# Batch 1 of an attention and MLP kernel: another split of k's subtraction, casts of v ahead of k's exponentials, products half a block later, batch 3's v loaded ahead of its q

## The chip, the cores and the metric

The kernel runs on one core of one Trainium2 chip. The metric is the device time of one execution in microseconds (us). The engines are named as the profile names them: PE multiplies matrices (PEld is its loading of weights), DVE is VectorE, ACT is ScalarE, POOL is GpSimd, and SP is SyncE, which here only issues transfers.

## What is computed

Linear attention on q, k and v of 8 batches, 8 heads, 576 rows and 64 columns, and a two-layer perceptron on its output:

```python
q_s = exp(q - max(q, axis=-1));  q_s = q_s / sum(q_s, axis=-1)
k_s = exp(k - max(k, axis=2));   k_s = k_s / sum(k_s, axis=2)     # axis 2: the rows
kv   = einsum('bhsd,bhse->bhde', k_s, v)
attn = einsum('bhsd,bhde->bhse', q_s, kv)
x    = attn, (batch, row) as 4608 tokens, (head, column) as 512 features
h    = x @ w_in                    # 512 to 2048
out  = maximum(0.01 * h, h) @ w_out  # 2048 to 512
```

The inputs are float32; the kernel multiplies in bfloat16 and writes float32.

## The kernel before, in words

**The perceptron sets the rhythm.** The 4608 tokens are worked in nine tiles of 512. In each tile, PE makes 16 blocks j of the first layer (L547, a block of 128 hidden features out of four matmuls), ScalarE takes each through the leaky function (L556), and PE makes the second layer (L568) for four groups of 128 tokens, 16 matmuls each. In tile 0 the second layer runs block by block: for each j one matmul for each of the four groups (L837 to L840).

**The attention of the next batches is put between these blocks by hand.** `at(t, u, fns)` hangs functions on step u of tile t, `run(t, u)` calls them there. In tile 0, u = 0 to 31 are blocks of the first layer and u = 32 + j is the end of block j of the second. In the other tiles, u = 0 to 15 are the blocks of the first layer, and from 16 on there is a step after every four matmuls of the second. An engine works in the order in which its instructions were emitted, so the hooks fix each engine's queue; semaphores do the rest. Where several functions are hung on one step, they go in the order of the `at` lines.

**One batch.** The rows of k, q and v are loaded by SP (L81) into one of six buffers `raw`, taken in turn: a load into a buffer waits until its last tile has been read. A batch's four column groups of heads are numbered 0 to 3; H0 is the first pair, H1 the second.
- k: `k_tree` and `k_allmax` make the maximum over the rows on VectorE (L153 to L178), `k_sub` subtracts it in place (L186, on VectorE or POOL), and `k_exp` takes the exponential on ScalarE (L194).
- q: `q_max` on VectorE (L229), `q_sub` (L288, on POOL for batch 1), `q_exp` on ScalarE (L296), then `q_sum` (L305, L307) and `q_norm` (L312) on VectorE. A transfer on SP's queue turns the normalized q (L535, or `turn_next`, L541, for batch 1, whose turned q is the tile X).
- v: `v_cast` to bfloat16, on POOL (L206) or ScalarE (L204).
- `kv` multiplies k by v on PE (L325) into two parts gg = 0, 1; gg = 0 needs H0 of k and of v, gg = 1 needs H1. `kd_make` divides by the sum on VectorE (L345, L346). Then `attend...` multiplies the turned q by it (L461) and x is copied (L484, L530), as input of the next tile's first layer.

**Batch 1 before the change.** Its rows 0 to 6 of q (R7) and all of k and v are prepared in tile 0 in pairs of heads. On VectorE: the maxima of q and k, k's subtraction of H1 (L687), then sum, reciprocal and normalization of q's H0, then of its H1. On POOL: the subtraction of q's H0, of q's H1, then of k's H0. On ScalarE: the exponentials of q's H0 and H1, of k's H1, the cast of v's H0, the exponential of k's H0, the cast of v's H1. SP has, behind the two turns of q, batch 2's k, the two last rows of batch 1's q, batch 2's q and v (`next_loads`, L675), and then the eight stores of tile 0. `kv(1)` is hung on u = 44, the end of block 12 of the second layer, and `attend_next` on u = 46. Batch 3 is loaded by `load_all(3)` at step 2 of tile 1: k, q, v. In tile 1, batch 2 is prepared (L702 to L719); its turned rows 0 to 5 and batch 1's last two rows are wanted by the matmuls hung on step 27 of tile 1 (L719). Batch 3's casts of v stand on POOL at step 0 of tile 2 (L738).

Of the kernel before, what the change touches and what calls it, by code (L numbers as in the profile page):

```python
# [25 lines left out]
def kernel(  # L26
# [9 lines left out]
    nc = tc.nc  # L36
# [35 lines left out]
    def raw(name):  # L72
        return raw_pool.tile([P, HL, R, D], FP32, name=name, tag="raw")

    def load(src, b, name, cuts, t=None):
        t = raw(name) if t is None else t
        flat = src[b].rearrange("h s d -> (h s d)").rearrange(
            "(hl p r d) -> p hl r d", hl=HL, p=P, r=R
        )
        for hs, rs in cuts:  # L80
            nc.sync.dma_start(  # L81
                out=t[:, hs, rs].rearrange("p h r d -> p h (r d)"),
                in_=flat[:, hs, rs].rearrange("p h r d -> p h (r d)"),
            )
        return t

    ALLH, ALLR = slice(0, HL), slice(0, R)
# [3 lines left out]
    st = [{} for _ in range(B)]  # L91
# [91 lines left out]
    def k_sub(eng, b, hs):  # L183
        ks = st[b]["k"][:, hs]
        n = hs.stop - hs.start
        eng.tensor_tensor(  # L186
            out=ks,
            in0=ks,
            in1=st[b]["kall"][:, hs].unsqueeze(2).to_broadcast([P, n, R, D]),
            op=ALU.subtract,  # L190
        )

    def k_exp(b, hs):
        nc.scalar.activation(  # L194
            out=st[b]["ke"][:, :, hs].rearrange("p r h d -> p h r d"),
            in_=st[b]["k"][:, hs],
            func=AF.Exp,
        )

    def v_cast(eng, b, gg):  # L200
        o = vb2[b % 2][:, :, gg, :, 0:D].rearrange("p r h d -> p h r d")
        i = st[b]["v"][:, 2 * gg : 2 * gg + 2]
        if eng is nc.scalar:
            eng.copy(out=o, in_=i)  # L204
        else:
            eng.tensor_copy(out=o, in_=i)  # L206


    def q_cols(b, rs, hs):
        if b != 1:  # L210
            return st[b]["qe"][:, rs, hs]
        flat = st[b]["qe"].rearrange("p r h d -> p (r h d)")
        cut = R7.stop * 2 * D
        i = 2 if rs.start else hs.start // 2
        return flat[:, i * cut : (i + 1) * cut if i < 2 else R * HL * D].rearrange(
            "p (r h d) -> p r h d", h=hs.stop - hs.start, d=D
        )
# [8 lines left out]
    def q_max(b, rs, hs=ALLH):  # L226
        n, m = rs.stop - rs.start, hs.stop - hs.start
        st[b]["qmax", rs.start, hs.start] = o = small_pool.tile([P, HL, n], FP32, name="qmax")[:, 0:m]
        nc.vector.tensor_reduce(out=o, in_=st[b]["q"][:, hs, rs], axis=AX.X, op=ALU.max)  # L229
# [55 lines left out]
    def q_sub(eng, b, rs, hs=ALLH):  # L285
        n, m = rs.stop - rs.start, hs.stop - hs.start
        qs = st[b]["q"][:, hs, rs]
        eng.tensor_tensor(  # L288
            out=qs,
            in0=qs,  # L290
            in1=st[b]["qmax", rs.start, hs.start].unsqueeze(3).to_broadcast([P, m, n, D]),
            op=ALU.subtract,
        )

    def q_exp(b, rs, hs=ALLH):
        nc.scalar.activation(  # L296
            out=q_cols(b, rs, hs).rearrange("p r h d -> p h r d"),
            in_=st[b]["q"][:, hs, rs],
            func=AF.Exp,
        )  # L300

    def q_sum(b, rs, hs=ALLH):
        n, m = rs.stop - rs.start, hs.stop - hs.start
        qsum = small_pool.tile([P, n, HL], FP32, name="qsum")[:, :, 0:m]
        nc.vector.reduce_sum(out=qsum, in_=q_cols(b, rs, hs), axis=AX.X)  # L305
        st[b]["qrec", rs.start, hs.start] = qrec = small_pool.tile([P, n, HL], FP32, name="qrec")[:, :, 0:m]
        nc.vector.reciprocal(out=qrec, in_=qsum)  # L307

    def q_norm(b, rs, hs=ALLH):
        n, m = rs.stop - rs.start, hs.stop - hs.start  # L310
        qes = q_cols(b, rs, hs)
        nc.vector.tensor_tensor(  # L312
            out=qes,
            in0=qes,
            in1=st[b]["qrec", rs.start, hs.start].unsqueeze(3).to_broadcast([P, n, m, D]),
            op=ALU.mult,
        )


    def kv_quads(b, gg, outs, rs=ALLR):  # L320
        for r in range(R)[rs]:
            for hp in range(2):
                for hh in range(2):
                    rows = slice(hh * L, (hh + 1) * L)
                    nc.tensor.matmul(  # L325
                        outs[hh][hp * D : (hp + 1) * D, 0 : D + 1],
                        lhsT=st[b]["ke"][rows, r, 2 * gg + hp],
                        rhs=vb2[b % 2][rows, r, gg, hp, 0 : D + 1],
                        start=(r == 0),
                        stop=(r == R - 1),  # L330
                    )

    def kv(b, mid=lambda: None):

        pkv = [psB_pool.tile([P, 2, D + 2], FP32, name="pkv", tag=BANK_TAG) for _ in range(2)]
        for gg, fn in zip(range(2), (mid, lambda: None)):
            kv_quads(b, gg, [pkv[hh][:, gg] for hh in range(2)])
            fn()
        st[b]["pkv"] = pkv

    def kd_make(b):
        for hh in range(2):
            pkv = st[b]["pkv"][hh]
            krec = small_pool.tile([P, 2, 1], FP32, name="krec")
            nc.vector.reciprocal(out=krec, in_=pkv[:, :, D : D + 1])  # L345
            nc.vector.tensor_tensor(  # L346
                out=kd2[b % 2][:, :, hh],
                in0=pkv[:, :, 0:D],
                in1=krec.to_broadcast([P, 2, D]),
                op=ALU.mult,  # L350
            )
# [73 lines left out]
    def q_transpose(b, r0, n, pool=psB_pool, tag=BANK_TAG):  # L425
        ps = pool.tile([P, NB, n, L], BF16, name="psum_qt", tag=tag)
        for rr in range(n):
            for gg in range(2):
                nc.tensor.matmul(
                    ps[:, gg::2, rr],  # L430
                    lhsT=st[b]["qe"][:, r0 + rr, 2 * gg : 2 * gg + 2].rearrange(
                        "p h d -> p (h d)"
                    ),
                    rhs=ident,
                    is_transpose=True,
                    start=(rr == 0 and gg == 0),
                    stop=(rr == n - 1 and gg == 1),
                )
        st[b]["ps", r0] = ps

    def q_keep(eng, b, r0, n, gs=slice(0, 4)):
        o, i = st[b]["qT"][:, gs, r0 : r0 + n], st[b]["ps", r0][:, gs]
        if eng is nc.scalar:
            eng.copy(out=o, in_=i)
        else:
            eng.tensor_copy(out=o, in_=i)
# [120 lines left out]
    def layer2(pout, g_sb, tsub, j, os=slice(0, O)):  # L567
        nc.tensor.matmul(  # L568
            pout,
            lhsT=g_sb[j // 2][:, j % 2, tsub * P : (tsub + 1) * P],  # L570
            rhs=w_out_sb[:, j, os],
            start=(j == 0),
            stop=(j == NF - 1),
        )
# [4 lines left out]
    def at(t, u, *fns):  # L579
        while t > 0 and u >= 32:  # L580
            t, u = t + 1, u - 32
        hooks.setdefault((t, u), []).extend(fns)

    def run(t, u):
        for fn in hooks.pop((t, u), ()):
            fn()

    H0, H1 = slice(0, 2), slice(2, 4)

    def load_all(b):  # L590
        whole = [(ALLH, ALLR)]
        st[b]["k"] = load(k, b, "k_raw", whole)
        st[b]["q"] = load(q, b, "q_raw", whole)
        st[b]["v"] = load(v, b, "v_raw", whole)

    held = const_pool.tile([1, 1, 128], BF16)

# [86 lines left out]
    at(0, 20, lambda: k_begin(1), lambda: q_begin(1), lambda: k_tree(1, H0), lambda: k_tree(1, H1))  # L684
    at(0, 20, lambda: q_max(1, R7, H0), lambda: q_sub(nc.gpsimd, 1, R7, H0), lambda: k_allmax(1))
    at(0, 20, lambda: q_max(1, R7, H1), lambda: q_sub(nc.gpsimd, 1, R7, H1))
    at(0, 20, lambda: k_sub(nc.vector, 1, H1), lambda: k_sub(nc.gpsimd, 1, H0))  # L687
    at(0, 27, more_loads)
    at(0, 31, lambda: q_exp(1, R7, H0), lambda: q_sum(1, R7, H0), lambda: q_norm(1, R7, H0))
    at(0, 31, lambda: q_exp(1, R7, H1), lambda: q_sum(1, R7, H1), lambda: q_norm(1, R7, H1))  # L690
    at(0, 31, lambda: k_exp(1, H1), lambda: v_cast(nc.scalar, 1, 0), lambda: k_exp(1, H0))
    at(0, 32, next_loads)
    at(0, 32, lambda: v_cast(nc.scalar, 1, 1))
    at(0, 44, lambda: kv(1), lambda: kd_make(1))
    at(0, 45, lambda: q_transpose(0, 8, 1), lambda: q_keep(nc.scalar, 0, 8, 1))
    at(0, 46, attend_next)
    at(1, 8, lambda: q_exp(1, RE))

    XR = (slice(0, 6), slice(6, R))
    at(1, 2, lambda: load_all(3))  # L700

    def plan2():  # L702
        b = 2
# [44 lines left out]
    for t in range(3, B - 1):  # L748
        b = t + 1
# [87 lines left out]
    for j in range(NF):  # L837
        for tsub in range(NTS):
            layer2(pout[tsub], g_sb, tsub, j)
        run(0, 32 + j)  # L840
    for tsub in range(NTS):
        store(tsub * P, pout[tsub])
# [57 lines left out]
```

## Time and profile before

| | us |
|---|---|
| median of 3 runs | 281.81 (281.69 to 282.1) |
| profiled execution | 282.38 |
| its span, first to last instruction | 280.6 |
| PE busy in it | 274.4 |
| granted clock of PE, share of full speed | 0.999 |

The span is what the page and the timelines cover, counted from its first instruction. A timeline line has the start in us, the duration in us, the engine, the line of the kernel, the operation, the tiles (written <- read), shapes, the number of instructions merged, and in brackets the idle time in front and what ended it. An instruction's duration includes what it waits for once it has started, a port for instance. A line of the transfers' view has the tile, the queue, the number, its KB and the median of the us from issue to landing; where it is one transfer, that is its own time. The tiles' borders in the trace: the second layer of tile 0 begins at 31.07 us, tile 1 at 47.3, its second layer at 61.3 and tile 2 at 76.6.

### The profile page before, as it was taken

The page shows a single profiled execution, that of the slowest core. Times are in us where ns is not written, and L with a number is a line of the kernel's source. Part 1 is how long each engine was busy: PE and PEld are TensorE (multiplying, and loading weights), DVE is VectorE, ACT ScalarE, POOL GpSimd, SP SyncE. Part 2 cuts the span into 40 slices and gives each one's busy share as a digit, 9 for nine tenths or more (in the row PEclk, how much of TensorE's full clock was granted, in tenths as well). Part 3 has the DMA queues.
Part 4 walks back from the last instruction along what each step waited for, and adds up shares of the span by engine and source line. Part 5 has one row for each costly group of instructions (what it writes and reads, how often), then busy time and mean ns, then how long its engine had stood idle before and what let it go on. Part 6 is the DMA issues. An engine that isn't in the chain of part 4 may idle for free.

```text
span 280.6 us, 4880 instructions
## 1 busy us (share of the span) xinstructions
PE 274.4 (98%) x1956; PEld 133.2 (47%) x1956; DVE 160.2 (57%) x227; ACT 159.5 (57%) x283; POOL 52.8 (19%) x54
## 2 busy tenths in 40 slices
PE   8899999999999999999999999999999999999994
PEld 3478644444444454445444544454444444444443
DVE  2986895999999969956795598644610000000021
ACT  4976554794489186755586448644844364146400
POOL 2947380156504002100500070000000000000000
PEclk9999999999999999999999999999999999999999
DMA  7999998989992299099309930333033300330033
GB/s 253 321 210 323 246 242 251 391 272 353 259 393 90 66 321 356 2 258 400 86 0 290 370 80 2 84 77 74 1 86 75 68 6 2 75 75 0 2 75 75
DMA packets 39606, 46.38 MB, mean 165 GB/s; under 512 B 18464, under 2 KB 22816, under 8 KB 39584
## 3 DMA queue, kind: packets, MB, share of 16 engines
q1 hardware_dynamic: 36064, 41.75, 47.8%
q0 software_dynamic: 3360, 4.20, 8.6%
q8 instruction: 15, 0.25, 0.3%
q10 hardware_dynamic: 160, 0.13, 0.1%
q14 instruction: 7, 0.06, 0.1%
HBM read 36.70 MB, written 9.44 MB: 164 GB/s over the span
## 4 chain that ended last, share of the span: by engine, by line
PE 83%; DMA 8%; POOL 4%; DVE 1%; SPq 1%; ACT 1%; issue 0%; DVEq 0%
PE pout L568 41%; PE ph L547 39%; DMA q_raw<-in_q_dram 3%; DMA w_in_sb<-in_moe_w_in_dram 2%; DMA k_raw<-in_k_dram 2%; POOL k_raw L186 1%; PE po L461 1%; SPq L81 1%; PE pokv L325 1%; POOL q_raw L288 1%; DVE qmax L229 1%; POOL w_in_sb L126 1%; PE pkv L325 1%; ACT ke L194 0%; POOL vb L206 0%
## 5 line engine op out<-in xcount | busy, mean ns | idle before, releaser
L568 PE MATMUL pout<-w_out_sb,gj 128*128 128x512 bf16 (+2 forms) x592 | 127.7, 373 | 0.0
L547 PE MATMUL ph<-xT,w_in_sb 128*128 128x512 bf16 (+1 forms) x640 | 126.6, 358 | 0.2 <-DMA w_in_sb<-in_moe_w_in_dram 0.2
L556 ACT ACTIVATE gj<-ph 128x512 bf16<-128x512 f32 x144 | 81.9, 601 | 25.7 <-PE ph L547 25.3
L547 PEld LDWEIGHTS <-w_in_sb 128*128 128x128 bf16 x640 | 62.3, 98 | 62.4 <-DMA w_in_sb<-in_moe_w_in_dram 0.5
L568 PEld LDWEIGHTS <-gj 128*128 128x128 bf16 x592 | 56.4, 98 | 65.4 <-issue 0.2
L562 ACT COPY out_sb<-pout 128x512 f32<-128x512 f32 (+1 forms) x29 | 16.8, 580 | 67.0 <-PE pout L568 39.7
L562 DVE COPY out_sb<-pout 128x512 f32<-128x512 f32 (+1 forms) x8 | 4.8, 635 | 70.8 <-PE pout L568 70.8
L206 POOL CAST vb<-v_raw 128x1152 bf16<-128x1152 f32 x13 | 23.7, 1850 | 80.3 <-DMA v_raw<-in_v_dram 57.5
L305 DVE TENSOR_REDUCE qsum<-qe 128x36 f32<-128x2304 bf16 (+5 forms) x13 | 20.0, 1542 | 10.4 <-ACT qe L296 10.3
L194 ACT ACTIVATE ke<-k_raw 128x1152 bf16<-128x1152 f32 (+2 forms) x12 | 17.8, 1482 | 9.6 <-DVE k_raw L186 9.1
L312 DVE TENSOR_TENSOR qe<-qe,qrec 128x2304 bf16<-128x2304 bf16 (+5 forms) x13 | 21.6, 1665 | 0.5
L296 ACT ACTIVATE qe<-q_raw 128x2304 bf16<-128x2304 f32 (+5 forms) x13 | 17.1, 1317 | 6.9 <-POOL q_raw L288 5.9
L229 DVE TENSOR_REDUCE qmax<-q_raw 128x36 f32<-128x2304 f32 (+5 forms) x13 | 19.9, 1537 | 0.7 <-DMA q_raw<-in_q_dram 0.7
L186 DVE TENSOR_TENSOR k_raw<-k_raw,kall 128x1152 f32<-128x1152 f32 (+1 forms) x9 | 17.3, 1940 | 0.3
L153 DVE TENSOR_TENSOR t<-t 128x256 f32<-128x256 f32 (+2 forms) x22 | 15.6, 711 | 0.7
L288 POOL TENSOR_TENSOR q_raw<-q_raw,qmax 128x512 f32<-128x512 f32 (+3 forms) x7 | 11.8, 1680 | 20.8 <-DVE qmax L229 19.1
L484 ACT CAST xT<-po 128x448 bf16<-128x448 f32 (+3 forms) x34 | 14.4, 517 | 1.1 <-PE po L461 1.1
L288 DVE TENSOR_TENSOR q_raw<-q_raw,qmax 128x2304 f32<-128x2304 f32 (+1 forms) x6 | 13.2, 2202 | 0.3
L153 DVE TENSOR_TENSOR t<-k_raw 128x512 f32<-128x512 f32 (+1 forms) x11 | 12.1, 1102 | 1.3 <-DMA k_raw<-in_k_dram 1.0
L345 DVE RECIPROCAL krec<-pokv 128x2 f32<-128x2 f32 x8 | 1.3, 164 | 19.6 <-PE pokv L461 19.6
L357 PE MATMUL pout<-zero 128*128 128x512 f32 (+3 forms) x18 | 9.5, 656 | 1.0 <-POOL zero L100 1.0
L325 PEld LDWEIGHTS <-ke 64*64 64x64 bf16 x504 | 5.9, 107 | 4.2 <-issue 2.8
(68 smaller groups left out, 107.2 us busy)
## 6 DMA issues: line engine op xcount, KB each, us to landing
out_dram<-out_sb SPq DMA_DIRECT2D x70, 128.0 KB, 2.5
q_raw<-in_q_dram SPq DMA_DIRECT2D x6, 1152.0 KB, 8.6
v_raw<-in_v_dram SPq DMA_DIRECT2D x6, 1152.0 KB, 11.4
k_raw<-in_k_dram SPq DMA_DIRECT2D x5, 1152.0 KB, 6.3
k_raw<-in_k_dram SPq DMA_DIRECT2D x6, 576.0 KB, 5.8
v_raw<-in_v_dram SPq DMA_DIRECT2D x4, 576.0 KB, 7.5
w_in_sb<-in_moe_w_in_dram POOLq DMA_DIRECT2D x8, 256.0 KB, 7.7
w_out_sb<-in_moe_w_out_dram POOLq DMA_DIRECT2D x6, 256.0 KB, 9.3
```

Of the source, the lines that this page charges most:

```text
L153: nc.vector.tensor_tensor(out=o, in0=i0, in1=i1, op=ALU.max)
L186: eng.tensor_tensor(out=ks, in0=ks, in1=st[b]["kall"][:, hs].unsqueeze(2).to_broadcast([P, n, R, D]), op=ALU.subtract,)
L194: nc.scalar.activation(out=st[b]["ke"][:, :, hs].rearrange("p r h d -> p h r d"), in_=st[b]["k"][:, hs], func=AF.Exp,)
L206: eng.tensor_copy(out=o, in_=i)
L229: nc.vector.tensor_reduce(out=o, in_=st[b]["q"][:, hs, rs], axis=AX.X, op=ALU.max)
L288: eng.tensor_tensor(out=qs, in0=qs, in1=st[b]["qmax", rs.start, hs.start].unsqueeze(3).to_broadcast([P, m, n, D]), op=ALU.subtract,)
L305: nc.vector.reduce_sum(out=qsum, in_=q_cols(b, rs, hs), axis=AX.X)
L312: nc.vector.tensor_tensor(out=qes, in0=qes, in1=st[b]["qrec", rs.start, hs.start].unsqueeze(3).to_broadcast([P, n, m, D]), op=ALU.mult,)
L547: nc.tensor.matmul(ph, lhsT=w_in_sb[:, cb, j * P : (j + 1) * P], rhs=xT[:, cb, c0 : c0 + n], start=(cb == 0 and first), stop=(cb == NB - 1 ...
L556: nc.scalar.activation(out=o, in_=ph, func=AF.Prelu, alpha=LEAKY_SLOPE)
L562: copy(out=out_sb, in_=pout)
L568: nc.tensor.matmul(pout, lhsT=g_sb[j // 2][:, j % 2, tsub * P : (tsub + 1) * P], rhs=w_out_sb[:, j, os], start=(j == 0), stop=(j == NF - 1),)
```

## The change

For batch 1, k's subtraction changes engines between the pairs: POOL now takes H1 and VectorE takes H0, and VectorE's stands behind the normalization of q's H0 and not ahead of q's sums. On ScalarE the casts of v go ahead of k's exponentials: cast H0, exponential H0, cast H1, exponential H1. `kv(1)` and `kd_make(1)` move from the end of block 12 of the second layer to the middle of block 13, by a new call of `run` after the second of the four matmuls: two matmuls later. And batch 3's loads go k, v, q, so v and q also change buffers; batches 4 to 7 keep k, q, v.

```diff
-    def load_all(b):
-        whole = [(ALLH, ALLR)]
-        st[b]["k"] = load(k, b, "k_raw", whole)
-        st[b]["q"] = load(q, b, "q_raw", whole)
-        st[b]["v"] = load(v, b, "v_raw", whole)
+    def load_all(b, order="kqv"):
+        for name in order:
+            st[b][name] = load(dict(q=q, k=k, v=v)[name], b, f"{name}_raw", [(ALLH, ALLR)])
...
-    at(0, 20, lambda: k_sub(nc.vector, 1, H1), lambda: k_sub(nc.gpsimd, 1, H0))
+    at(0, 20, lambda: k_sub(nc.gpsimd, 1, H1))
     at(0, 27, more_loads)
     at(0, 31, lambda: q_exp(1, R7, H0), lambda: q_sum(1, R7, H0), lambda: q_norm(1, R7, H0))
+    at(0, 31, lambda: k_sub(nc.vector, 1, H0))
     at(0, 31, lambda: q_exp(1, R7, H1), lambda: q_sum(1, R7, H1), lambda: q_norm(1, R7, H1))
-    at(0, 31, lambda: k_exp(1, H1), lambda: v_cast(nc.scalar, 1, 0), lambda: k_exp(1, H0))
+    at(0, 31, lambda: v_cast(nc.scalar, 1, 0), lambda: k_exp(1, H0))
     at(0, 32, next_loads)
-    at(0, 32, lambda: v_cast(nc.scalar, 1, 1))
-    at(0, 44, lambda: kv(1), lambda: kd_make(1))
+    at(0, 32, lambda: v_cast(nc.scalar, 1, 1), lambda: k_exp(1, H1))
+    at(0, 44.5, lambda: kv(1), lambda: kd_make(1))
...
-    at(1, 2, lambda: load_all(3))
+    at(1, 2, lambda: load_all(3, "kvq"))
...
             layer2(pout[tsub], g_sb, tsub, j)
+            if tsub == 1:
+                run(0, 31.5 + j)
         run(0, 32 + j)
```

## The prediction

> **What bounds the kernel now.** I read the page's busy table first, then the waits of PE, then the engines' timelines from 34 to 47 us, where the change lies.
>
> ```profile
> PE 274.4 (98%) x1956; PEld 133.2 (47%) x1956; DVE 160.2 (57%) x227; ACT 159.5 (57%) x283; POOL 52.8 (19%) x54
> ```
>
> PE is busy for 274.4 of 280.6 us, and of its waits over 0.15 us after 25 us one is left, in batch 1's key-value products (L325). The timeline of PE shows it (start, duration, engine, line):
>
> ```profile
> 40.78 1.67 PE L568 MATMUL pout<-w_out_sb,gj 128*128 128x512 bf16 x7
> 42.47 0.48 PE L325 MATMUL pkv<-vb,ke 64*64 64x65 bf16 x36
> 43.51 0.48 PE L325 MATMUL pkv<-vb,ke 64*64 64x65 bf16 x36 [0.56 <-ACT vb L204]
> ```
>
> So 0.56 us, 0.2% of the time, is all that a perfect change here can win. Who makes ScalarE late is in the timelines of POOL, VectorE and ScalarE:
>
> ```profile
> 35.05 2.73 POOL L288 TENSOR_TENSOR q_raw<-q_raw,qmax 128x896 f32<-128x896 f32 x1 [1.45 <-DVE qmax L229]
> 37.75 3.47 POOL L186 TENSOR_TENSOR k_raw<-k_raw,kall 128x1152 f32<-128x1152 f32 x1
> ...
> 34.89 1.35 DVE L186 TENSOR_TENSOR k_raw<-k_raw,kall 128x1152 f32<-128x1152 f32 x1
> 36.16 1.08 DVE L305 TENSOR_REDUCE qsum<-qe 128x14 f32<-128x896 bf16 x1
> 37.27 0.24 DVE L307 RECIPROCAL qrec<-qsum 128x14 f32<-128x14 f32 x1
> 37.55 1.19 DVE L312 TENSOR_TENSOR qe<-qe,qrec 128x896 bf16<-128x896 bf16 x1
> ...
> 40.20 1.98 DVE L312 TENSOR_TENSOR qe<-qe,qrec 128x896 bf16<-128x896 bf16 x1
> ...
> 38.67 1.15 ACT L194 ACTIVATE ke<-k_raw 128x1152 bf16<-128x1152 f32 x1
> 39.73 1.14 ACT L204 CAST vb<-v_raw 128x1152 bf16<-128x1152 f32 x1
> 41.25 1.16 ACT L194 ACTIVATE ke<-k_raw 128x1152 bf16<-128x1152 f32 x1 [0.38 <-POOL k_raw L186]
> 42.32 1.14 ACT L204 CAST vb<-v_raw 128x1152 bf16<-128x1152 f32 x1
> ```
>
> The reader is to see that VectorE's TENSOR_TENSOR and POOL's run by turns. The same 896-wide normalization takes 1.19 and 1.98 us; each ends 0.95 us after the POOL instruction in front of it (37.78 to 38.73, 41.22 to 42.17). POOL's subtraction of q took 1.68 us at 31.92, beside reductions, and 2.73 here, ending 1.54 after VectorE's subtraction (36.24). So this stretch is one chain of turns: 1.2 (k on VectorE), 1.54 (q on POOL), 0.95, 2.49 (k on POOL, 38.73 to 41.22), 0.95.
>
> **Who gets the turn.** In batch 5's maxima on VectorE, beside its casts on POOL:
>
> ```profile
> 110.46 1.41 POOL L206 CAST vb<-v_raw 128x1152 bf16<-128x1152 f32 x1 [22.14 <-DMA v_raw<-in_v_dram]
> ...
> 110.90 1.25 DVE L153 TENSOR_TENSOR t<-t 128x256 f32<-128x256 f32 x1
> ```
>
> The cast was waiting when a VectorE instruction ended at 110.86, and ran before VectorE's next, which alone takes 0.42 (at 88.89) and here 1.25. POOL's back-to-back casts at 63.61 and 64.70 likewise let a VectorE instruction in between. No row shows a VectorE instruction that needs nothing of the one before it following directly while POOL waits: the changed order has just that.
>
> **The change, part by part.** Times up to 34.97, the end of the second maximum of q, stay.
>
> 1. VectorE no longer subtracts k there: it goes straight to q's first sum (34.89 to 35.97, by 1.08) and reciprocal (to 36.24). POOL's q subtraction starts at 35.05 as before and is alone: 1.68, to 36.73. The normalization waits for it and ends 0.95 later, 37.68. ScalarE's second q exponential, 37.82 before, starts at 36.77 and ends at 37.72.
>
> 2. POOL's k subtraction (heads 2, 3 now) has waited since 36.7; VectorE's (heads 0, 1) is issued at 37.6, behind the normalization. **Here the forecast parts.**
>    - Case A, turns alternate: POOL 37.68 + 2.49 = 40.17; VectorE 1.21 more (the 58.16 row ends 1.21 after POOL's 58.77), 41.38. Behind it in VectorE's queue stand q's second sum (1.08), reciprocal (0.24) and normalization (0.95): 43.66 instead of 42.17, +1.49.
>    - Case B, VectorE keeps the turn: 37.68 + 1.21 = 38.89, POOL to 41.38, second normalization 0.95 later, 42.33, +0.16. It is not earlier than before in either: the turns are the same work in another order.
>
>    I take A, by the 110.90 row, the nearest. The Trainium skill, "SBUF — State Buffer", section "Who interferes with whom", says that a VectorE instruction with two SBUF inputs and a GpSimd one that reads SBUF exclude each other for whole instructions, and that issue order decides who blocks; the waits above agree (0.95 us behind POOL's end, twice). By that rule the POOL subtraction, issued first, goes first: the sum of A, not of B.
>
> 3. ScalarE. The v halves land at 37.6 and 40.45 (issued 30.22 and 30.64; 7.4 and 9.8 us to landing). Case A: first cast 37.7 to 38.8, heads 0, 1 wait for VectorE and run 41.42 to 42.57 (1.15), second cast to 43.6 (it stands behind that exponential, its data long there), heads 2, 3 to 44.67. Case B: 38.8, 40.1, 41.6, 42.7.
>
> 4. The products go two L568 matmuls later (run at 31.5 + 13 = 44.5): 42.47 + 2 × 0.22 = 42.91, second half 43.39. Moving them costs nothing by itself; matmuls only change places. Case A: the second half waits for heads 2, 3 from 43.39 to 44.69, 1.30 against 0.56: **+0.74**. Case B: no wait, −0.56. What follows stays covered in both: VectorE's L345/L346 take 0.9 us behind the products and the next user is 1.4 us behind (0.44 + 0.11 + 0.86); the second transposed q (2.6 us from issue) lands at 46.3 (A) or 45.0 (B), wanted at 46.8 or 45.5.
>
> 5. The queue of SP. Behind the second transpose, which waits for the second normalization, SP issues batch 2's k, the rest of batch 1's q, batch 2's q and v, and the stores. All of them move by +1.49 or +0.16. The DMA engines are then full (391 GB/s from 46 to 57 us, share 1.04), and SP issued batch 3's k at 58.14, behind a store that went out as batch 2's v landed (57.56): the shift is handed on. It is paid where PE takes up the next transposes:
>
> ```profile
> qX<-qe SPq DMA_TRANSPOSE x1, 5.6
> X<-qe SPq DMA_TRANSPOSE x1, 3.7
> ...
> 72.41 0.52 PE L461 MATMUL po<-qX,kd 64*64 64x384 bf16 x8
> 72.76 0.28 PE L461 MATMUL po<-X,kd 64*64 64x128 bf16 x8
> ```
>
>    Issued at 66.44 and 68.92, they land at 72.06 and 72.60, behind batch 3's last load (59.37 + 11.3 = 70.69), for matmuls at 72.41 and 72.76. The slack is 0.16 us, less a start of some 0.08 (30.65 landed, 30.74 used, on VectorE): 0.08. So X starts at 72.76 + shift − 0.08 at the earliest, whatever PE won before. Case A: +1.41, more than the 0.74. Case B: +0.08: the 0.56 is given back. The Trainium skill, "DMA: Bandwidth & Descriptors", section "Issuing engines are not separate DMA queues", says that all issues share the same 16 DMA engines, so no other queue would help; here the landing 1.4 us behind the last load agrees.
>
> 6. Batch 3's v before its q: two equal loads (1152 KB) change places and the last still lands where it did, so the transposes gain nothing. v comes at about 67.2 instead of 70.69, and POOL's casts move onto VectorE's normalization of 69.09; one cast in front of it costs it 0.75. Then L345/L346 end at 71.6, not 70.86, still before 72.4, and the maxima from 70.78, slowed by 0.83 twice now, run free. q lands at 70.7 and is wanted at 80.09. **Nothing**, bounded by −0.2 and +0.2. If that cover were gone, 0.75.
>
> From 73 on PE has no wait and the nearest slack I found is 1.7 us (exponential of heads 0, 1 at 98.91 to 100.07, used at 101.79).
>
> **Sum.** Case A: +1.4. The profiled execution took 282.38 us, span 280.6 and 1.8 around it; the median of the plain runs is 281.81. I add the difference to the median: 283.2.
>
> **Rivals.**
> - Case B, VectorE keeps the turn and the loads pass on their 0.16: 281.81 + 0.08 = 281.9, no change. For it: the two instructions need nothing of each other, and VectorE starts such a one 0.07 before the end in front (59.91 against 59.98). Against: POOL's back-to-back casts did not keep the turn.
> - Faster: VectorE keeps the turn, and X lands at 72.2 or earlier because its landing doesn't hang on the loads before it. Place: the wait of PE at 72; price −0.56; it decides from a landing 0.4 us earlier. 281.3. Against: all three transposes of that place land in a row behind the load.
> - Case A without the hand-on: only the products' wait, +0.74, 282.6.
> - The v ahead of q might decide by itself, casts delaying kd_make to the matmuls at 72.4: 0.75 at the most and only if VectorE has no slack, which it has (0.8).
>
> **How the numbers follow.** Case A with the hand-on 0.40, without it 0.17, Case B 0.30, the faster one 0.10, other 0.03. What a measurement of this kernel can tell is about 0.2%, 0.56 us. Faster by more than that is the limit of the only wait, so 0.09; Case B and its neighbours within 0.2%: 0.34; slower: 0.57. The range takes in Case B with −0.4 around it and A with +0.3: 281.4 to 283.5. The forecast's own range is 282.5 to 283.5.
>
> **What would show it.** Right: POOL's k subtraction ends near 40.2 and VectorE's near 41.4; PE waits 1.3 us for ke; SP issues the second transpose near 43.7; PE waits again near 73. Wrong: VectorE's subtraction ends near 38.9, PE has no wait at L325; then the time hangs on whether X lands behind 72.2.

## The result, and the profile after

| | before | changed |
|---|---|---|
| median | 282.19 (10 runs) | 283.82 (282.6 to 285.41, 10 runs) |
| profiled execution | 282.38 | 284.4 |
| its span | 280.6 | 282.6 |

The ratio is 1.006, with a 95% interval of 1.0036 to 1.0083: slower by 1.6 us. One run of the kernel before, at 410.3 us, is a disturbed one and left out of the ratio. The forecast was 283.2, by +1.4 on a median of 281.81, with 281.4 to 283.5 as range; 283.82 lies 0.3 above the range. In the longer series the kernel before stands at 282.2 to 282.3, which is 0.4 of the difference to the forecast; the other 0.2 are the change's.

The busy line of the page, then PE's waits after 20 us (waiting tile and line, what ended it, us in total, times, longest):

```profile
PE 273.4 (97%) x1956; PEld 133.0 (47%) x1956; DVE 160.4 (57%) x227; ACT 159.7 (57%) x283; POOL 48.8 (17%) x54
```

```profile
PE pkv L325 <- ACT ke L194: 1.3, 1, 1.3
PE po L461 <- DMA X<-qe: 1.1, 1, 1.1
```

One wait of 0.56 us has become two, 1.3 and 1.1. The timelines of POOL, VectorE and ScalarE of the changed kernel show the first one's cause:

```profile
34.91 1.69 POOL L288 TENSOR_TENSOR q_raw<-q_raw,qmax 128x896 f32<-128x896 f32 x1 [1.46 <-DVE qmax L229]
36.55 3.47 POOL L186 TENSOR_TENSOR k_raw<-k_raw,kall 128x1152 f32<-128x1152 f32 x1
```

```profile
36.13 1.41 DVE L312 TENSOR_TENSOR qe<-qe,qrec 128x896 bf16<-128x896 bf16 x1
37.47 3.77 DVE L186 TENSOR_TENSOR k_raw<-k_raw,kall 128x1152 f32<-128x1152 f32 x1
...
42.55 1.09 DVE L312 TENSOR_TENSOR qe<-qe,qrec 128x896 bf16<-128x896 bf16 x1
```

```profile
41.27 1.16 ACT L194 ACTIVATE ke<-k_raw 128x1152 bf16<-128x1152 f32 x1 [2.40 <-DVE k_raw L186]
42.34 1.14 ACT L204 CAST vb<-v_raw 128x1152 bf16<-128x1152 f32 x1
43.38 1.16 ACT L194 ACTIVATE ke<-k_raw 128x1152 bf16<-128x1152 f32 x1
```

VectorE's subtraction of k takes 3.77 us and not 1.35. It starts at 37.47, as the normalization ends (37.54); POOL's, whose record begins at 36.55, runs first, to 40.02, and VectorE's ends 1.22 later. The last exponential ends at 44.54. PE's timeline then reads:

```profile
42.82 0.48 PE L325 MATMUL pkv<-vb,ke 64*64 64x65 bf16 x36
44.59 0.48 PE L325 MATMUL pkv<-vb,ke 64*64 64x65 bf16 x36 [1.29 <-ACT ke L194]
...
46.76 0.20 PE L461 MATMUL po<-qT,kd 64*64 64x64 bf16 x4
48.03 0.38 PE L461 MATMUL po<-X,kd 64*64 64x448 bf16 x4 [1.07 <-DMA X<-qe]
```

1.29 against 0.56 is +0.73, and 1.07 more for X, the turned q: 1.8 of the 2.0 us between the two spans. The second turn (the transfer that turns q's second half) was issued at 43.70. The transfers' view gives its us to landing, first in the kernel before, then in the changed one:

```profile
X<-qe SPq DMA_TRANSPOSE x1, 2.6
```

```profile
X<-qe SPq DMA_TRANSPOSE x1, 4.3
```

In the transfers of 45.7 to 46.0 us stands something that is no transfer of the kernel, a packet of instructions (queue, kind, packets, MB, share). That they are PE's shows below, where instructions put on PE alone move it:

```profile
q8 instruction: 1, 0.02, 22.4%
```

It is one packet of 16,384 bytes, begun at 45.81 and 1.08 us long. The turn's transfer has 32 packets of 4 bytes at its end: 30 of them start from 45.67 to 45.85, the other two at 46.87 and 46.88, as the fetch ends. Of its 16 completions, fifteen came from 46.16 to 46.30 and the last at 47.99. In the kernel before the same fetch began at 44.74, 0.35 us after the turn's last packet (44.38), here in the transfers of 44.7 to 44.8:

```profile
q8 instruction: 1, 0.02, 101.2%
```

### The profile page after: what moved, and what is told of

Its sections match the earlier page's. It is cut to its first block, busy times and chain, and to the rows that moved or that the text cites. A ratio compares the mean times of both kernels' runs of the same rounds, so it can differ in the third digit from the quotient of the medians.

```text
span 282.6 us, 4880 instructions
## 1 busy us (share of the span) xinstructions
PE 273.4 (97%) x1956; PEld 133.0 (47%) x1956; DVE 160.4 (57%) x227; ACT 159.7 (57%) x283; POOL 48.8 (17%) x54
## 4 chain that ended last, share of the span: by engine, by line
PE 82%; DMA 9%; DVE 4%; POOL 2%; SPq 1%; issue 1%; ACT 0%; DVEq 0%
PE pout L568 40%; PE ph L547 39%; DMA q_raw<-in_q_dram 4%; DMA w_in_sb<-in_moe_w_in_dram 2%; DMA k_raw<-in_k_dram 2%; DMA X<-qe 2%; DVE k_raw L186 1%; PE po L461 1%; PE pokv L325 1%; DVE qmax L229 1%; POOL w_in_sb L126 1%; SPq L81 1%; PE pkv L325 1%; DVE qe L312 0%; ACT vb L204 0%
## 5 line engine op out<-in xcount | busy, mean ns | idle before, releaser
L206 POOL CAST vb<-v_raw 128x1152 bf16<-128x1152 f32 x13 | 20.9, 1636 | 83.7 <-DMA v_raw<-in_v_dram 83.7
L186 DVE TENSOR_TENSOR k_raw<-k_raw,kall 128x1152 f32<-128x1152 f32 (+1 forms) x9 | 19.7, 2209 | 0.3
L288 POOL TENSOR_TENSOR q_raw<-q_raw,qmax 128x512 f32<-128x512 f32 (+3 forms) x7 | 10.7, 1531 | 23.3 <-DVE qmax L229 21.6
L153 DVE TENSOR_TENSOR t<-t 128x256 f32<-128x256 f32 (+2 forms) x22 | 13.2, 599 | 0.7
L357 PE MATMUL pout<-zero 128*128 128x512 f32 (+3 forms) x18 | 8.2, 574 | 1.0 <-POOL zero L100 1.0
```

The lines of the kernel that those rows point to most:

```text
L153: nc.vector.tensor_tensor(out=o, in0=i0, in1=i1, op=ALU.max)
L186: eng.tensor_tensor(out=ks, in0=ks, in1=st[b]["kall"][:, hs].unsqueeze(2).to_broadcast([P, n, R, D]), op=ALU.subtract,)
L288: eng.tensor_tensor(out=qs, in0=qs, in1=st[b]["qmax", rs.start, hs.start].unsqueeze(3).to_broadcast([P, m, n, D]), op=ALU.subtract,)
```

## The experiments

Theories: **(T1)** a waiting POOL subtraction goes ahead of VectorE's (the turns, Case A). **(T2)** The fetch of PE's instructions holds up a turn whose packets it meets. **(T3)** The shift of batch 2's loads is handed on to the turned q wanted at 72 us. Rivals: the order on ScalarE or the later place of the products (against T1), the loads issued right behind the turn (against T2), slack at 72 us (against T3). Ratios are to the kernel before, measured beside each (median 282.23 or 282.28), with 95% intervals.

**Batch 3's order alone**, in the kernel before:

```diff
-    at(1, 2, lambda: load_all(3))
+    at(1, 2, lambda: load_all(3, "kvq"))
```

> The kernel before, with batch 3's loads as k, v, q and nothing else changed. Theory (the order of two equal loads has no price): same time as before, within 0.3 us; the turned q of the step at 72 us lands within 0.3 us of 72.1 and 72.6. Rival (batch 3's casts on POOL move onto VectorE's normalization and delay what the matmuls at 72 us need): 0.5 to 0.75 us slower, with a wait of PE there.

Measured: 282.09, ratio 0.9998 (0.9983 to 1.0013); X landed at 72.09 for 72.60. No price, as forecast. Its profile shows something else: the kernel is the same as before up to 48 us, and yet PE has no wait for another engine at the products. VectorE's second maximum of q ended at 34.47, not 34.97, since the loads of q ahead of it had landed 0.5 to 0.6 us earlier. The wait of 0.56 us that the forecast started from is one execution's.

**VectorE first**: POOL reads one element of VectorE's result ahead of its own subtraction.

```diff
-    at(0, 20, lambda: k_sub(nc.gpsimd, 1, H1))
...
     at(0, 31, lambda: k_sub(nc.vector, 1, H0))
+    at(0, 31, lambda: nc.gpsimd.tensor_copy(out=gate[:, 0:1], in_=st[1]["k"][:, 1, R - 1, D - 1 : D]))
+    at(0, 31, lambda: k_sub(nc.gpsimd, 1, H1))
```

> The changed kernel, where POOL reads one element of VectorE's result ahead of its own subtraction of k, so that VectorE's subtraction of heads 0, 1 has the turn and POOL's comes behind it. Theory (the changed kernel is late because POOL, waiting longer, takes the port ahead of VectorE): VectorE's subtraction takes 1.2 to 1.4 us and not 3.77, the wait of PE at the products falls from 1.3 us to under 0.2, the second normalization ends near 42.4, and the time is 0.0 to 0.3 us above the kernel before, up to 1.0 if the instruction fetch of PE falls on the turn of q. Rival (the order of casts and exponentials on ScalarE or the later place of the products made it slow): the wait stays near 1.3 us and the time at 1.4 or more above.

VectorE's timeline and POOL's, of this kernel:

```profile
37.08 1.35 DVE L186 TENSOR_TENSOR k_raw<-k_raw,kall 128x1152 f32<-128x1152 f32 x1
...
39.73 2.53 DVE L312 TENSOR_TENSOR qe<-qe,qrec 128x896 bf16<-128x896 bf16 x1
```

```profile
38.55 0.18 POOL L688 COPY gate<-k_raw 128x1 f32<-128x1 f32 x1 [2.34 <-issue]
38.69 2.63 POOL L186 TENSOR_TENSOR k_raw<-k_raw,kall 128x1152 f32<-128x1152 f32 x1
```

1.35 instead of 3.77, the second normalization ends at 42.26, and the wait at the products is gone: T1 holds, and its rival falls. The time did not come back as cleanly: 283.36, ratio 1.0026 (1.0002 to 1.0051), in two groups, five runs of 281.6 to 282.5 and seven of 283.4 to 285.4. The profiled execution was in the first (281.98).

**VectorE at its old place**, still with heads 0, 1, all else as changed:

```diff
-    at(0, 20, lambda: k_sub(nc.gpsimd, 1, H1))
+    at(0, 20, lambda: k_sub(nc.vector, 1, H0), lambda: k_sub(nc.gpsimd, 1, H1))
...
-    at(0, 31, lambda: k_sub(nc.vector, 1, H0))
```

> The changed kernel with VectorE's subtraction (still of heads 0, 1) back at its place ahead of q's sums; casts ahead of exponentials, products half a block on and batch 3's order stay. Theory of the turns and of the hand-on: second normalization ends within 0.2 us of the kernel before's, no wait at the products (0.56 us won there), and the gain is given back at 72 us, where the turned q lands at 72.6 as before: within 0.2 us of the kernel before, up to 0.7 above it if the instruction fetch falls on the turn of q. Rival (the loads do not bind the step at 72 us): 0.4 to 0.6 us faster than before.

Measured: 281.81, ratio 0.999 (0.9976 to 1.0004); no wait at the products, span 280.0. So it is the place behind the first pair that costs, neither the exchange of heads nor ScalarE's order. The giving back that was expected at 72 us is not in this profile: X landed at 71.48, not at 72.6, and PE did not wait. The interval holds the theory's time and the rival's.

**The later products alone**, in the kernel before (with the new call of `run`):

```diff
-    at(0, 44, lambda: kv(1), lambda: kd_make(1))
+    at(0, 44.5, lambda: kv(1), lambda: kd_make(1))
```

> The kernel before with the products two matmuls later and nothing else of the change. Theory: the cast of v's second half ends at 43.46, the second half of the products is reached at 43.39, so the wait falls from 0.56 to about 0.1 us: 0.3 to 0.5 us faster than before, if the step at 72 us has slack in most executions. Rival (the turned q of the step at 72 us binds, as the prediction had it): within 0.15 us of the kernel before, with a wait for qX or X there. If the instruction fetch of PE meets the second turn of q: 0.5 to 1 us slower in some runs.

Measured: 281.94, ratio 0.9993 (0.9981 to 1.0005), span 280.2, no wait at the products or at 72 us, where X landed at 72.28. The times exclude neither reading: the interval holds both 0.15 and 0.5 us of gain. This and the kernel in front are the fastest tried, and neither is measurably faster than before. Their only waits after 25 us are these:

```profile
PE pout L568 <- issue: 0.3, 2, 0.2
```

These are two pauses of 0.16 us, one right behind batch 1's products (43.9) and one near 94.5 us, in which nothing in the profile holds PE. The profile before and the first one of the changed kernel have neither; later profiles have them also where PE waits 1.0 us at the products. What makes them stays open.

**The fetch moved**, in the changed kernel, by 180 empty instructions on PE's sequencer at the start.

```diff
-    wake(TT, TT, TT, 256)
+    for n in (TT, TT, TT, 256):
+        wake(n)
+        for _ in range(45):
+            nc.tensor.nop(hint="pad", nofuse=True)
```

> The changed kernel with 180 empty instructions of PE's sequencer between the first warm-up matmuls, so that PE's 16 KB instruction fetch that fell at 45.81 us, on top of the second turn of q, comes several us earlier. Theory (the fetch held up the last of the 16 completions of that turn, 47.99 us against 46.30 for the other fifteen): the turn lands 2.6 us after its issue, PE's wait of 1.1 us for X goes, the wait of 1.3 us for ke stays, and the time is 0.7 to 1.3 us above the kernel before, 0.5 or more below the changed kernel's 1.6. Rival (batch 2's loads, issued right behind, held it up): it lands 4.3 us after its issue, the wait of 1.1 us stays, 1.6 to 2.0 us above the kernel before.

Measured: 291.98, ratio 1.0353. They cost some 50 ns each (45 of them 2.3 us from one matmul to the next). The second layer of tile 0 began 8.7 us late, at 39.73, so that PE came to the products and to X after both were ready. The turn landed 2.6 us after its issue, with no fetch within 4 us of it; the time says nothing.

**The fetch moved, at less cost**: 114 of them in PE's pauses up to 14 us, in the changed kernel and, as control, in the kernel before; `skip(n)` emits n of them.

```diff
-    wake(TT, TT, TT, 256)
+    skip(16)
+    for n, m in ((TT, 16), (TT, 16), (TT, 16), (256, 8)):
+        wake(n)
+        skip(m)
...
+    skip(14)   # and 8, 10, 10 behind the next warm-up matmuls
```

> The changed kernel with 114 empty sequencer instructions on PE, spread over the pauses of its first 14 us (at some 50 ns each, at most 17 behind one warm-up matmul of 0.85 us), so that PE's 16 KB instruction fetch comes some 2.5 us earlier than 45.81. Theory (the fetch holds up the last completion of the second turn of q): the turn lands 2.6 us after its issue, PE's wait for X near 47 us goes, the wait of 1.3 us for ke stays; 0.4 to 1.0 us above the kernel before, 0.6 to 1.2 below the changed kernel, and less spread between runs than its 2.8 us. Rival (batch 2's loads, issued right behind the turn, hold it up): 4.3 us to landing, the wait of 1.1 us stays, 1.6 above the kernel before. If the empty instructions themselves cost time, the control run (the same in the kernel before) shows how much.

> The kernel before with the same 114 empty sequencer instructions on PE. Control: their own cost is 0 to 0.5 us (PE's early pauses hide them); the turned q of batch 1 lands 2.6 us after its issue as before, and the wait of 0.56 us at the products stays. If it is 1 us or more slower, the run beside it is to be read against this one.

Changed: 285.16, ratio 1.009 (1.0064 to 1.0117). Control: 284.31, ratio 1.0068 (1.0041 to 1.0095). In the control, PE's first matmul starts 1 us later, and the fetch now falls at 43.81, onto the turn's packets in the kernel before, where it had not been and was not expected. The transfers' view, first of the turn in the control, then in the changed kernel with the fetch at 43.33, ahead of the turn's packets:

```profile
X<-qe SPq DMA_TRANSPOSE x1, 4.3
```

```profile
X<-qe SPq DMA_TRANSPOSE x1, 2.8
```

So a fetch put on the turn makes it late in the kernel before, and one taken off it makes it timely in the changed kernel (its packets begin at 44.60, as the fetch ends), with batch 2's loads issued 0.1 us behind the turn in either. That is T2. The second half is the weaker one, since three of the four unaltered profiles of the changed kernel have a timely turn too (table below); the control and the packets' times carry it. Both expectations of the time missed, and neither time is a price of the late turn. In the changed kernel the next fetch went to 72.21, while the next turn was under way, which took 7.5 us to land and cost PE a wait of 1.7. In the control's profile PE waits 0.3 us for X, so most of its 2.0 us is not the late turn and stays unexplained.

**Loads held** until the turn has landed, in the changed kernel:

```diff
+        hold_sync(0, st[1]["X1"][0:1, 13])
         st[2]["k"] = load(k, 2, "k_raw", [(H0, ALLR), (H1, ALLR)])
```

> The changed kernel, where SP issues batch 2's loads only when the second turn of q has landed (a 256-byte copy of its last block stands in front of them). Theory (PE's instruction fetch holds up the last completion): the turn is late as often as in the changed kernel, by up to 1.7 us, although no load is behind it; batch 2's loads come 3 to 5 us later; the time is 1.5 to 4 us above the kernel before. Rival (the loads behind it hold it up): it lands 2.6 us after its issue in the profile and PE has no wait for X near 47 us; what is left is the 1.3 us for ke and what the later loads cost.

Measured: 285.74, ratio 1.0124 (1.0084 to 1.0164). Its profile has the turn on time (2.6), but the fetch begins at 46.31, behind its packets, so it doesn't part T2 from its rival; a turn on time is what the rival expected. It does show T3. PE's waits:

```profile
PE po L461 <- DMA qX<-qe: 1.5, 1, 1.5
PE pkv L325 <- ACT ke L194: 1.2, 1, 1.2
PE pkv L325 <- POOL vb L206: 1.0, 1, 1.0
```

Batch 2's k was issued at 47.29 and not 43.55, +3.74; X of the step at 72 us landed at 76.49 and not 72.60, +3.89; the span is 284.3, +3.7.

**More profiles** of the changed kernel and of the one with VectorE first, both unaltered, one execution each.

> The changed kernel once more, unaltered, for a second profile. Theory (whether PE's 16 KB instruction fetch overlaps the second turn of q decides between its fast and slow executions, 282.6 to 285.4 us): if the fetch begins before the turn's data have gone, the turn lands over 4 us after its issue, PE waits about 1 us for X, and the span is 282 or more; if it begins after, the turn lands 2.6 us after its issue, no wait for X there, and the span is 280.8 to 281.6. Rival (something else makes the difference): span and landing do not go together. The wait of 1.3 us for ke and VectorE's subtraction of 3.8 us are there in either.

> The changed kernel a third time, unaltered. Same expectation as for the second profile: span and landing of the second turn of q go together, by the place of the instruction fetch.

> The kernel in which VectorE's subtraction has the turn, once more, unaltered; its times fell into two groups, 281.6 to 282.5 and 283.4 to 285.4. Theory: in the first group the fetch comes behind the turn (as in its profile, 44.68 against data gone at 44.5), in the second it overlaps, the turn lands 4 us or more after its issue and PE waits 1 to 1.5 us for X near 46 us. Rival: in the second group the time is lost elsewhere, with the turn on time.

> The same kernel a third time, unaltered, with the same expectation.

> The kernel in which VectorE's subtraction has the turn, unaltered, one more look. Theory: if its time is above 283, the fetch overlaps the second turn of q, which lands over 4 us after its issue, and PE waits over 1 us for X near 46 us; if it is under 282.5, the turn is on time. Rival: above 283 with the turn on time, the loss elsewhere (a wait at 72 us, or none that shows).

> The kernel in which VectorE's subtraction has the turn, unaltered, another look, with the same two readings: over 283 us with the second turn of q late (theory) or on time (rival).

> The kernel in which VectorE's subtraction has the turn, unaltered, a further look, with the same two readings: over 283 us with the second turn of q late (theory) or on time (rival).

> The changed kernel, unaltered, one more look. Theory: a time above 283.5 goes with a second turn of q that lands over 4 us after its issue and a wait of PE for X near 47 us; one below goes with 2.6 us and none. Rival: time and landing do not go together.

All profiles with PE's instructions in their old places, this study's first ones too, in order of the time from the issue of the second turn to the start of the fetch (us):

| kernel, profile | issue to fetch | issue to landing | PE's wait for X | span |
|---|---|---|---|---|
| VectorE first, h1 | 1.98 | 4.1 | 1.5 | 281.4 |
| changed, first | 2.11 | 4.3 | 1.1 | 282.6 |
| changed, loads held | 2.26 | 2.6 | none | 284.3 |
| VectorE first, g4 | 2.31 | 2.6 | none | 280.6 |
| changed, g1 | 2.31 | 2.6 | none | 281.4 |
| changed, g2 | 2.33 | 2.6 | none | 281.4 |
| VectorE first, first | 2.35 | 2.6 | none | 280.2 |
| batch 3's order alone | 2.36 | 2.6 | none | 280.1 |
| VectorE first, h3 | 2.36 | 4.4 | 1.3 | 281.2 |
| VectorE first, g3 | 2.39 | 2.6 | none | 279.9 |
| before | 2.50 | 2.6 | none | 280.6 |
| old place | 2.57 | 2.6 | none | 280.0 |
| VectorE first, h2 | 2.57 | 2.6 | none | 280.4 |
| later products alone | 2.65 | 2.6 | none | 280.2 |
| changed, h4 | 2.94 | 2.6 | none | 281.3 |

Up to 2.11 the turn is late, from 2.50 it is on time; between 2.26 and 2.39 it is a race, and one of eight was late. The control above, at 1.78, was late too. The two late profiles of VectorE first (283.2 and 283.04 us) are the slowest of its six: landing and span go together, as T2 has it. A late turn has two forms. In the first profile and in h3 the last two packets of 4 bytes alone came behind the fetch, and one completion of 16 was late. In h1 and the control 5 and 23 of the turn's 896 packets of 256 bytes also came behind it, and then all 16 completions were late. PE's waits in h1, in g4, and in g1, a changed kernel with a timely turn:

```profile
PE po L461 <- DMA X<-qe: 1.5, 1, 1.5
```

```profile
PE po L461 <- DMA qX<-qe: 0.7, 1, 0.7
```

```profile
PE pkv L325 <- ACT ke L194: 1.0, 1, 1.0
PE pout L568 <- issue: 0.3, 2, 0.2
PE po L461 <- DMA qX<-qe: 0.2, 1, 0.2
```

In g4 the turn was timely, nothing waited at the products, and 0.7 us were given back at 72 us, so that the span is that of before (280.6). This shows that the step at 72 us can bind, but not that a later issue made it: batch 2's k was issued at 43.51 in g4 and at 43.54 in g3, and X landed at 72.72 and 71.68. In the fifteen profiles of the table X landed 28.1 to 29.2 us behind the issue of batch 2's k. So the shift is handed on, but with 1.1 us of scatter, against the 1.47 us (43.55 to 45.02) by which the change shifts that issue.

## Why the prediction was right or wrong

1. **Case A, turns alternate: right.** The forecast for the ends of VectorE's subtraction, POOL's and the second normalization was 41.4, 40.2 and 43.66; 41.24, 40.02 and 43.64 were measured. VectorE first and the old place show that it is this and not ScalarE's order or the later products.
2. **The wait at the products: right.** 1.30 was forecast and 1.29 measured in the first profile; the three others of the changed kernel, whose second maximum of q ends 0.3 to 0.4 us earlier than in the first, have 0.8 to 1.0.
3. **The hand-on of the loads: right in kind, but it was not what bound the first profile.** The forecast had X land at 74.1 (72.60 + 1.49) and PE wait for it near 73; X landed at 73.62, and PE, late already by the two waits at 44 and 48 us, took it up at 74.80 without a wait. The three profiles with a timely turn have X at 73.38 to 73.54 and spans of 281.3 to 281.4. Their chain on VectorE starts 0.5 us earlier than in the profile before (second maximum to 34.40 in g1, 34.97 before). Three kernels without the shift that start within 0.2 us of them (batch 3's order alone, old place, later products alone) have X at 72.09, 71.48 and 72.28 and spans of 280.0 to 280.2: X lands 1.1 to 2.1 us later with the shift (forecast 1.49), and the span is 1.1 to 1.4 longer (forecast 1.41). Of this, 0.8 to 1.0 is the wait at the products; at 72 us PE waits 0.3 at most (g1, for qX and X).
4. **Wrong: the landing of the second turned q**, part 4: "the second transposed q (2.6 us from issue) lands at 46.3 (A)". It landed at 47.99 in the first profile and cost 1.07 us where cover was assumed, a term that the sum put at nothing and the range did not hold. I took the duration of a transfer from an execution in which PE's fetch fell 0.35 us clear of it, and moved the transfer by 1.5 us and PE by 0.7. In three of four profiles of the changed kernel the turn was on time, and these took 283.08 to 283.23 us, inside the range; the fourth, with the late turn, took 284.4. How often the turn was late in the unprofiled runs is not known. Of the ten times, the profiled 284.4 among them, three are 282.6 to 282.95, two 283.53 and 283.62, and five 284.03 to 285.41; that late turns lift the median of 283.82 is argued from this and not shown.
5. **That +1.4 came near the measured +1.6 is in part luck.** In the first profile the +2.0 of the span is 0.73 at the products and 1.07 for the late turn, and nothing at the step of 72 us, which set the forecast's +1.41.
6. **Batch 3's order: right,** no price (0.9998).
7. Case B's account holds as well: with VectorE first, the timely executions span 279.9 to 280.6. That its ratio is still 1.0026 may be the late turn again, which Case B's 281.9 did not have either; but the two late profiles took 283.04 and 283.2, and the seven slower ones of its runs 283.35 to 285.4, so this is not shown.
8. The limit of 0.56 us for a gain was the wait of one execution: the run with batch 3's order alone, the same up to 48 us, has no such wait.

Not settled: which of the 16 DMA engines the fetch takes, and so what decides the race between 2.26 and 2.39 us; the records don't name the engine.

## What to carry to other kernels

Where instructions of two engines run by turns, as VectorE's and POOL's do here, an instruction put behind another on the same engine loses its place to whatever already waits on the other one: look for what has been waiting longest. Before a step is moved, ask what else runs at the place where it lands, PE's instruction fetches included, whose places can be read from the transfers' records. And a slack or a wait taken from one profile should be looked up in a second: half a microsecond here was the start of one execution.

## What the runs showed of the hardware

- PE's instructions come in packets of 16,384 bytes over the DMA engines, 0.9 to 2.0 us each, and the rest of a transfer that meets one comes as the fetch ends: the turn's last two packets at 46.87 and 46.88, the fetch's end at 46.88, fifteen completions to 46.30 and the sixteenth at 47.99. The Trainium skill, "Runtime: NRT & Kernel Launch", section "Instruction fetch mechanics", says that the sequencer fetches the next 16 KiB page by a DMA queue of its own and that the crossing is mostly hidden; the size agrees, and PE works on without a gap while the fetch runs (45.81 to 46.88), but the transfer beside it lands 1.5 to 1.8 us late. The Trainium skill, "DMA: Bandwidth & Descriptors", section "Why a DMA increments its semaphore by 16 and not by 1", says that the engines of a DMA finish independently and the semaphore counts them; the 15 and 1 agree, in the first profile and h3, while in h1 and the control all 16 came late together (46.78 to 46.87, 46.26 to 46.33).
- An empty instruction on PE's sequencer took some 50 ns (45 of them in 2.3 us).
- VectorE gives way to a waiting POOL even when its next instruction needs nothing of the one before and its record starts 0.07 us ahead of that one's end (37.47 against 37.54; 3.77 us for a subtraction of 1.35).
